# A tuned attention-and-expert kernel: one transpose moved from TensorE to DMA, one conversion moved ahead, loads issued one pair sooner, the last output split over two banks

## Chip, cores, metric

One core of one Trainium2 chip. The metric is device microseconds of one launch. The kernel before takes 212.0 us (median of 3 runs, 211.11 to 213.35). The profiled execution of it has a span of 209.9 us and took 211.65 us, so about 1.8 us lie outside the span.

A run is called slow here if it took over 1.5% more than the fastest run of the same kernel. Ratios are the mean time of one kernel's fast runs over that of the other's fast runs of the same rounds, so they are not quite the ratio of the medians that I quote.

## The reference, cut to what matters

```python
# q, k, v: 4 batches x 8 heads x 768 steps x 64
for t in range(S):
    state = gamma * state + k[:, :, t] (x) v[:, :, t]
    y[:, :, t] = scale * q[:, :, t] @ state
x = y.transpose(0, 2, 1, 3).reshape(3072, 512)
h = x @ w_in                     # 512 x 2048
out = (h * cos(h)) @ w_out       # 2048 x 512
```

## The kernel before

The 768 steps are cut into 6 chunks of 128. A *pair* p is one chunk of two batches; there are 12 pairs (p = 0 to 11; the "fourth pair" is p = 3). Two pairs make one group g of 512 tokens for the two large products. The parts that matter:

```python
SLOT = [0, 1, 2, 3, 2, 4, 0, 1, 3, 2, 4, 0]      # buffers of q, k, v by pair

def conv_q(p, eng): ...    # q * decay -> bf16, on VectorE or GpSimd
def conv_k(p, True): ...   # k -> bf16, on ScalarE
def conv_v(p, eng): ...    # v * decay -> bf16

def stage_t(p, b):         # 8 TensorE transposes into a PSUM bank, one VectorE copy
def stage_t_dma(p):        # the same by DMA, issued from SP
    for b in range(2):
        nc.sync.dma_start_transpose(out=qkt[n][:, b]..., in_=qk[n][:, b]...)

def attend(p):             # scores: matmuls on the transposed q and k (L215), then mask (L223)
def stage_y(p):            # outputs and state of the pair (L236, L241, L257)
def pair_f / unit_f        # x @ w_in, cosine on ScalarE, product on VectorE (L296, L284)
def unit_o(g, j, part)     # @ w_out (L310), copied by ScalarE, sent by SP

# ... pairs 2 and 3:
conv_k(2, True); conv_q(2, nc.vector)
#     ... stage_t(2, 0); stage_t(2, 1); conv_v(2, nc.vector); attend(2) between unit_o ...
conv_k(3, True); conv_q(3, nc.gpsimd)
load(nc.sync, 4, ("q0", "q1"));       load(nc.gpsimd, 4, ("k0", "k1", "v0", "v1"))
conv_v(3, nc.gpsimd)
load(nc.sync, 5, ("q0", "q1", "v0")); load(nc.gpsimd, 5, ("k0", "k1", "v1"))
#     ... stage_t(3, 0); stage_t(3, 1); attend(3) ...
stage_t_dma(4); load(nc.sync, 6, q); load(nc.gpsimd, 6, k and v)
#     ... stage_t_dma(5) ...
def later(p):
    stage_y(p)
    if p + 3 < NP: load(nc.sync, p + 3, q); load(nc.gpsimd, p + 3, k and v)
```

q goes out on SP's queue, k and v on GpSimd's. Pairs 0 to 3 are transposed by TensorE, pairs 4 to 11 by DMA.

## Time and profile before

| what | before |
|---|---|
| time, span | 212.0 us, 209.9 us |
| TensorE busy | 202.4 us (96%) |
| TensorE waits on a DMA of qkt (the transposed q and k) | none |
| DMA transposes | 16, 2.7 to 8.7 us from issue to landing |
| granted clock | 1.00 |

In the views below, a line of waits reads: engine and line, what it waited for, us in total, times, longest us. A timeline line reads: start, duration, engine, line, operation, count, and in brackets the idle time before it and what ended it. "SPq" is SP issuing a DMA: its duration is the time of issuing, not of the transfer. A DMA-issue line gives the count and the median us from issue to landing. In a line of stretches come the stretch, its length, busy us (and instructions) of TensorE, its weight loads, VectorE, ScalarE and GpSimd, then the granted clock, the DMA share and GB/s.

### The profile page before, as it was taken

Reading aid. Unit: us, or ns where it says so; the run is one execution under the profiler, and the core shown is the slowest. Engines: PE = TensorE matmul, PEld = TensorE weight load, DVE = VectorE, ACT = ScalarE, POOL = GpSimd, SP = SyncE. Lnnn points to the kernel's source line nnn. Section 1 sums busy time; section 2 is a strip of 40 time slices with the busy share of each in tenths; the row PEclk is TensorE's granted clock in tenths of the full one; section 3 lists DMA queues with packets and bytes.
Section 4 is the critical chain, followed back from the end, with each engine's and each line's share of the span. In section 5 each row is a group of like instructions: output and inputs, shape, how many; then the busy total and the mean of one; then the engine's idle time right before and its main releaser. Section 6 shows DMA issues by size and latency. Waiting matters only on the chain.

```text
span 209.9 us, 4164 instructions
## 1 busy us (share of the span) xinstructions
PE 202.4 (96%) x1637; PEld 112.3 (54%) x1637; DVE 115.5 (55%) x190; ACT 111.8 (53%) x181; POOL 91.4 (44%) x105
## 2 busy tenths in 40 slices
PE   7799999999999999999999999999999999999992
PEld 3258554548898555555455455455455444444440
DVE  4694785372967746859585385385482333443000
ACT  6267783227898337766845735735545554553120
POOL 7998238499995952999980700000000000000000
PEclk9999999999999999999999999999999999999999
DMA  6999999999799999999999171181101101110121
GB/s 154 340 247 207 216 260 288 338 265 349 177 217 237 218 307 283 182 290 227 288 115 273 53 103 52 50 103 50 50 3 50 50 4 50 50 50 27 74 88 65
DMA packets 49124, 33.83 MB, mean 161 GB/s; under 512 B 40080, under 2 KB 42384, under 8 KB 49104
## 3 DMA queue, kind: packets, MB, share of 16 engines
q1 hardware_dynamic: 42192, 15.86, 34.5%
q0 software_dynamic: 6768, 17.57, 31.8%
q8 instruction: 13, 0.21, 0.4%
q10 hardware_dynamic: 144, 0.13, 0.2%
q14 instruction: 7, 0.06, 0.1%
HBM read 27.26 MB, written 6.29 MB: 160 GB/s over the span
## 4 chain that ended last, share of the span: by engine, by line
PE 89%; POOL 3%; DMA 3%; DVE 2%; issue 1%; ACT 0%; POOLq 0%; DVEq 0%
PE bank L310 39%; PE bank L284 32%; PE bank L296 9%; DMA w_in<-in_moe_w_in_dram 3%; PE bank L236 3%; PE bank L215 3%; PE bank L241 2%; POOL vf L113 2%; POOL kf L113 1%; PE st_ps L257 1%; DVE vs L168 1%; PE bank L189 1%; DVE qkt L179 1%; POOL qf L113 0%; DVE am L223 0%
## 5 line engine op out<-in xcount | busy, mean ns | idle before, releaser
L279 DVE TENSOR_TENSOR gt<-bank,cosb 128x512 bf16<-128x512 f32 x96 | 65.7, 690 | 64.1 <-ACT cosb L275 63.7
L275 ACT ACTIVATE cosb<-bank,halfpi 128x512 bf16<-128x512 f32 x96 | 65.6, 688 | 52.3 <-PE bank L284 46.7
L310 PE MATMUL bank<-w_out_sb,gt 128*128 128x512 bf16 x384 | 93.3, 379 | 0.0
L284 PE MATMUL bank<-xt,w_in 128*128 128x512 bf16 x304 | 75.1, 380 | 0.0
L310 PEld LDWEIGHTS <-gt 128*128 128x128 bf16 x384 | 36.7, 98 | 42.8
L284 PEld LDWEIGHTS <-w_in 128*128 128x128 bf16 x304 | 33.8, 114 | 30.8 <-issue 0.2
L223 DVE TENSOR_TENSOR am<-bank,mask 128x512 bf16<-128x512 f32 x48 | 30.2, 681 | 0.3 <-PE bank L215 0.2
L163 POOL TENSOR_TENSOR qk<-qf,gq 128x512 bf16<-128x512 f32 x18 | 18.7, 1061 | 17.9 <-DMA qf<-in_q_dram 15.7
L322 ACT COPY ob<-bank 128x512 f32<-128x512 f32 x23 | 13.4, 587 | 22.6 <-PE bank L310 22.5
L168 POOL TENSOR_TENSOR vs<-vf,gk 128x512 bf16<-128x512 f32 x22 | 22.5, 1044 | 0.1
L113 POOL DMA_DIRECT2D vf<-in_v_dram x23 | 20.3, 886 | 5.0 <-DMA w_out_sb<-in_moe_w_out_dram 5.0
L113 POOL DMA_DIRECT2D kf<-in_k_dram x23 | 20.8, 906 | 2.0 <-DMA w_out_sb<-in_moe_w_out_dram 1.2
L174 ACT CAST qk<-kf 128x512 bf16<-128x512 f32 x24 | 13.9, 615 | 11.4 <-DMA kf<-in_k_dram 11.2
L296 PE MATMUL bank<-xt,w_in 128*128 128x256 bf16 x160 | 18.7, 273 | 0.6 <-ACT xt L245 0.4
L296 PEld LDWEIGHTS <-w_in 128*128 128x128 bf16 x160 | 17.1, 114 | 1.4 <-DMA w_in<-in_moe_w_in_dram 0.5
L245 ACT CAST xt<-bank 128x512 bf16<-128x512 f32 x24 | 13.0, 587 | 3.0 <-DVE gt L279 3.0
L241 PE MATMUL bank<-am,vs 128*64 128x128 bf16 x192 | 11.8, 220 | 0.7 <-POOL vs L168 0.7
L241 PEld LDWEIGHTS <-vs 128*64 128x64 bf16 x192 | 9.9, 110 | 2.1 <-POOL vs L168 1.7
L236 PEld LDWEIGHTS <-stb 128*64 128x64 bf16 x160 | 8.6, 109 | 4.0 <-issue 3.5
L236 PE MATMUL bank<-qkt,stb 128*64 128x128 bf16 x160 | 10.6, 222 | 0.0
L262 DVE CAST stb<-st_ps 64x512 bf16<-64x512 f32 x12 | 8.2, 687 | 3.5 <-PE st_ps L257 3.3
L332 PE MATMUL bank<-gt 128*128 128x512 bf16 x21 | 8.4, 514 | 1.2 <-DVE gt L140 1.2
(36 smaller groups left out, 66.1 us busy)
## 6 DMA issues: line engine op xcount, KB each, us to landing
kf<-in_k_dram POOLq DMA_DIRECT2D x23, 256.0 KB, 6.0
vf<-in_v_dram POOLq DMA_DIRECT2D x23, 256.0 KB, 7.0
out_dram<-ob SPq DMA_DIRECT2D x23, 256.0 KB, 2.0
qf<-in_q_dram SPq DMA_DIRECT2D x19, 256.0 KB, 6.7
w_in<-in_moe_w_in_dram POOLq DMA_DIRECT2D x4, 512.0 KB, 7.8
w_out_sb<-in_moe_w_out_dram POOLq DMA_DIRECT2D x4, 512.0 KB, 12.3
qf<-in_q_dram POOLq DMA_DIRECT2D x5, 256.0 KB, 7.4
kf<-in_k_dram SPq DMA_DIRECT2D x1, 256.0 KB, 4.7
```

Source lines behind the costliest of these rows:

```text
L113: eng.dma_start(out=t[SLOT[p]][b], in_=src[2 * bp + b, :, ds(c * C, C)].rearrange("h t d -> t h d"))
L163: eng.tensor_tensor(out=qk[p % NB][:, b, 0], in0=qf[SLOT[p]][b], in1=bc(gq, p % NC), op=ALU.mult)
L168: eng.tensor_tensor(out=vs[p % NB][:, b], in0=vf[SLOT[p]][b], in1=bc(gk if g is None else g, p % NC), op=ALU.mult)
L174: nc.scalar.copy(out=qk[p % NB][:, b, 1], in_=kf[SLOT[p]][b])
L223: nc.vector.tensor_tensor(out=am[p % 2][b][j], in0=ap[j], in1=mask.unsqueeze(1).to_broadcast([128, HP, 128]), op=ALU.mult)
L236: nc.tensor.matmul(yp[ts(j, 64), a, :], lhsT=stb[p % 2][:, b, a, ts(j, 64)], rhs=qt(n, b, a), start=True, stop=False, skip_group_check=True)
L241: nc.tensor.matmul(yp[ts(j, 64), a, :], lhsT=vs[n][:, b, 2 * a + j, :], rhs=am[p % 2][b][j][:, a, :], start=(c == 0), stop=True, skip_grou ...
L275: nc.scalar.activation(out=cb, in_=bank, func=AF.Sin, bias=halfpi)
L279: nc.vector.tensor_tensor(out=out, in0=bank, in1=cb, op=ALU.mult)
L284: nc.tensor.matmul(bank, lhsT=w_in_t(i, f), rhs=xt[g % 2][:, i, :], start=(i == 0), stop=(i == KIN - 1))
L296: nc.tensor.matmul(bank[:, ts(e, 256)], lhsT=w_in_t(i, f + e), rhs=xt[g % 2][:, i, ts(hf, 256)], start=(i == 0 and e == 0), stop=(i == KIN ...
L310: nc.tensor.matmul(bank, lhsT=gt[g % 2][:, f, ts(j, 128)], rhs=w_out_sb[:, f, :], start=(f == 0), stop=(f == KOUT - 1))
```

## The change

The intent was to take work and waits off TensorE, and to give the loads more lead. Four parts:

```diff
 # part 4: the last output, in place of halves of one bank copied one after the other
+    def last_o(g, j):
+        for i, (a, n) in enumerate(((0, 320), (320, 192))):
+            bank = banks.take()
+            ... 16 matmuls of n columns ...
+            # i = 0: ScalarE copies, SP sends; i = 1: VectorE copies, ScalarE's queue sends
 # part 2: third pair's v ahead of its transposes
     conv_q(2, nc.vector)
+    conv_v(2, nc.vector)
...
-                conv_v(2, nc.vector)        # was behind stage_t(2, 1)
 # part 1: fourth pair by DMA
     conv_q(3, nc.gpsimd)
+    stage_t_dma(3)
     load(nc.sync, 4, ("q0", "q1"))
...
-    stage_t(3, 0)
-    stage_t(3, 1)
 # part 3: loads from the eighth pair on one pair sooner
     stage_t_dma(5)
+    load(nc.sync, 7, ("q0", "q1"))
+    load(nc.gpsimd, 7, ("k0", "k1", "v0", "v1"))
...
-        if p + 3 < NP:
-            load(nc.sync, p + 3, ("q0", "q1"))
-            load(nc.gpsimd, p + 3, ("k0", "k1", "v0", "v1"))
+        if p + 4 < NP:
+            load(nc.sync, p + 4, ("q0", "q1"))
+            load(nc.gpsimd, p + 4, ("k0", "k1", "v0", "v1"))
```

More of the change, by code (lines that the diff above doesn't have):

```diff
@@ L315, in unit_o @@
             dst = out[ds((2 * bp + j % 2) * S + c * C, C), :]
-            if g == NG - 1 and j == 3:
-                nc.vector.tensor_copy(out=o[:, ts(0, 256)], in_=bank[:, ts(0, 256)])
-                nc.sync.dma_start(out=dst[:, ts(0, 256)], in_=o[:, ts(0, 256)])
-                nc.scalar.copy(out=o[:, ts(1, 256)], in_=bank[:, ts(1, 256)])
-                nc.scalar.dma_start(out=dst[:, ts(1, 256)], in_=o[:, ts(1, 256)])
-            else:
-                nc.scalar.copy(out=o, in_=bank)
-                nc.sync.dma_start(out=dst, in_=o)
-            banks.give(bank)
+            nc.scalar.copy(out=o, in_=bank)
+            nc.sync.dma_start(out=dst, in_=o)
+            banks.give(bank)
+    def last_o(g, j):
+        bp, c = divmod(2 * g + j // 2, NC)
+        dst = out[ds((2 * bp + j % 2) * S + c * C, C), :]
+        for i, (a, n) in enumerate(((0, 320), (320, 192))):
+            bank = banks.take()
+            for f in range(KOUT):
+                nc.tensor.matmul(bank[:, :n], lhsT=gt[g % 2][:, f, ts(j, 128)],
+                                 rhs=w_out_sb[:, f, ds(a, n)],
+                                 start=(f == 0), stop=(f == KOUT - 1))
+            o = ob[i]
+            if i:
+                nc.vector.tensor_copy(out=o[:, :n], in_=bank[:, :n])
+                nc.scalar.dma_start(out=dst[:, ds(a, n)], in_=o[:, :n])
+            else:
+                nc.scalar.copy(out=o[:, :n], in_=bank[:, :n])
+                nc.sync.dma_start(out=dst[:, ds(a, n)], in_=o[:, :n])
     spare = banks.take()
@@ L472 @@
             if g > 2:
-                unit_o(g - 1, *divmod(s, 4))
+                if g < NG or s < 12:
+                    unit_o(g - 1, *divmod(s, 4))
+                elif s == 12:
+                    last_o(g - 1, 3)
             if p < NP:
```

## The prediction

> **What bounds the kernel now.** I read the page's busy line first, then the chain of waits, then TensorE's own waits, then the timeline of the stage that the change touches. The page says:
>
> ```profile
> span 209.9 us, 4164 instructions
> PE 202.4 (96%) x1637; PEld 112.3 (54%) x1637; DVE 115.5 (55%) x190; ACT 111.8 (53%) x181; POOL 91.4 (44%) x105
> PE 89%; POOL 3%; DMA 3%; DVE 2%; issue 1%; ACT 0%; POOLq 0%; DVEq 0%
> ```
>
> TensorE is busy for 96% of the span and holds 89% of the chain that ended last; no other engine is past 55%. The rest of the chain lies in three places: 15.6 us at the start (loads until w_in lands, which the change leaves alone), a VectorE piece between 40.0 and 44.0 us, and the end. So only TensorE work taken away, or TensorE waits taken away, can shorten this kernel. TensorE's waits, longest first, are few:
>
> ```profile
> PE bank L332 <- DVE gt L140: 1.2, 1, 1.2
> PE bank L241 <- POOL vs L168: 0.7, 1, 0.7
> PE bank L296 <- ACT xt L245: 0.4, 1, 0.4
> PE bank L215 <- DVE qkt L179: 0.4, 1, 0.4
> PE bank L215 <- DVE am L223: 0.4, 1, 0.4
> ...
> PE bank L296 <- DMA w_in<-in_moe_w_in_dram: 0.2, 1, 0.2
> ```
>
> From 60 us to 206.2 us the same view is empty. Whatever the change does to loads there can bring TensorE nothing; it can only take something away.
>
> The timeline of 36 to 60 us shows the third pair (p=2):
>
> ```profile
> 40.03 1.29 DVE L179 TENSOR_SCALAR qkt<-bank 128x512 uint32<-128x512 uint32 x2 [5.15 <-PE bank L189]
> 41.23 2.13 DVE L168 TENSOR_TENSOR vs<-vf,gk 128x512 bf16<-128x512 f32 x2
> 43.29 2.47 DVE L223 TENSOR_TENSOR am<-bank,mask 128x512 bf16<-128x512 f32 x4
> 43.39 0.23 PE L215 MATMUL bank<-qkt 64*128 64x128 bf16 x1
> 44.02 0.38 PE L215 MATMUL bank<-qkt 64*128 64x128 bf16 x7 [0.40 <-DVE am L223]
> ```
>
> VectorE copies the transposed q and k, then converts v for 2.13 us, and only then masks. The second batch's scores (L215) start at 43.39, and their second matmul waits to 44.02 for a bank that the mask frees. And the chain, listed in order of time, has the fourth pair's transposes as TensorE time of their own:
>
> ```profile
> 51.08 0.89 PE bank L189 x16
> ```
>
> **What the Trainium skill says.** "TensorE: Matmul & The Clock Gate", Part 4: PE-mode transpose: its output goes to PSUM, so a copy follows. Agreed: each batch's 8 transposes are followed by one L179 copy of 684 ns. Its figure of about 275 ns per transpose is not the cost in a stream; here 16 take 0.89 us, 56 ns each. "SBUF — State Buffer", Who interferes with whom: a VectorE instruction with two SBUF inputs contends with a GpSimd one that reads SBUF. Agreed: the two conversions of v on VectorE took 682 and 1533 ns, the longer while GpSimd converted q (1283 ns against a median of 1049). "PSUM — Partial Sum Buffer", PSUM bank collisions raise a hardware error: two engines may not touch one bank's quadrant at once, even reading. That is why the two halves of the last output are copied one after the other before; two banks allow both. "DMA: Bandwidth & Descriptors", DMA Transpose (X-bar): 2-byte data, from SP or ACT; both hold here. The trace gives the time: 2.8 to 8.0 us from issue to landing.
>
> **The change, part by part.**
>
> 1. Fourth pair by DMA. Goes: 16 transposes, 0.89 us of TensorE, all on the chain, and two VectorE copies (2 x 0.68 us) with no TensorE wait of their own. Comes: two DMA transposes ahead of the loads of pairs 4 and 5 on SP's queue. Their inputs: k converted at 41.2 us, q at 42.8 us. Needed: the fourth pair's scores ran at 53.7, so about 52.1 now. With 1.25 us per issue and the trace's 2.8 to 8.0 us they land at about 46 to 51: in time. **-0.89 us.**
>
> 2. v of the third pair ahead of T. v's two loads were issued at 26.46 and 29.37 and took 10.9 and 8.7 us: landed at 37.4 and 38.1. Two conversions of 0.68 us then end at about 38.8, before the transposes' copy at 40.03. The masks start right after the scores (about 41.6), two end by 43.0, and banks are free when TensorE comes at 43.4. From there to the next w_out group (44.40) it took 1.01 us where 8 score matmuls need 0.28 (half of 0.55 for 16). **-0.73 us.**
>
> 3. Loads sooner from the eighth pair on: no TensorE wait lies there, so **0**.
>
> 4. The last output in two banks, of 320 and 192 columns. TensorE: the same 16 x 512 columns at 0.42 ns each (3.46 us), as the weight loads stay hidden even at 128 columns (56 ns a transpose). Before: copy on VectorE from 206.23 to 206.67, copy on ScalarE from 206.69 to 207.06, then the last transfer is issued (207.09). After: the first bank is copied and sent while TensorE makes the second, and one VectorE copy of 192 columns is left (about 0.36 us, an estimate from 425 ns for 256 and 690 for 512). 0.86 - 0.40 = **-0.46 us.**
>
> Sum: 0.89 + 0.73 + 0.46 = 2.08 us, of 212.0: 209.9, or 1.0%.
>
> **The rivals.**
>
> *A: SP's queue falls behind, and pair 4's or 5's transpose arrives late.* Issues on SP keep their order. Before, pairs 4 and 5's q went out while SP had nothing else to do:
>
> ```profile
> 33.85 9.57 SPq L113 DMA_DIRECT2D qf<-in_q_dram  x4
> 43.46 0.78 SPq L113 DMA_DIRECT2D vf<-in_v_dram  x1
> 46.02 4.63 SPq L323 DMA_DIRECT2D out_dram<-ob  x4
> 55.02 3.47 SPq L198 DMA_TRANSPOSE qkt<-qk  x2
> ```
>
> They took 9.57 us to issue, for the queue was full (landing after 6 to 10 us, 16 engines at a share of 1.0 throughout). Now they stand behind a transpose that waits for pair 3's conversions until 41 to 43 us. Moved by 8 to 10 us, with the free stretch of 50.65 to 55.02 to absorb 4.4 of it and less competition from GpSimd's queue to absorb some more, pair 4's transpose goes out at 55 to 58 instead of 55.02. It landed at 61.5 and 64.5 (6.5 and 8.0 us), and pair 4's scores started at 66.39: 1.9 us of slack, of which parts 1 and 2 use 1.6. Pair 5 is alike: landed at 68.6 and 69.5, scores at 71.77. Any delay here becomes a TensorE wait before L215. For it: those numbers, and the busy DMA. Against: GpSimd's loads of pair 3 lose a competitor and come 1 to 2 us sooner, so the transpose of pair 3 too. I give a visible loss even odds, of 0.3 to 2 us, about 0.7 on average: 210.2 to 212.
>
> *B: v lands after the transposes are done.* VectorE works in order, so v landing past 39.4 would hold up the copy. In the trace it landed 1.3 us sooner. One chance in ten; up to 1 us lost, 210.9.
>
> *C: the extra transposes and earlier loads take DMA time from pairs 6 to 8.* Pair 6's transposes landed at 70.5 and 71.6 for scores at 79.59; pair 7's at 87.8 for 91.61; pair 8's at 100.6 for 104.89: 4 to 8 us of slack. Pair 7's q was what GpSimd waited 5.7 us for at 76 to 82, and that gets better. Unlikely to cost anything: 209.9.
>
> *D: the gain is larger, because waits that I count once ripple.* With no wait after 60 us, nothing is there to ripple: 209.5 at best.
>
> **Range and chances.** 209.9 if nothing is late, less than half a microsecond more for rival A on average: **210.2 us**. Low end 208.9: all parts, and a run as good as the lowest before (211.1 - 2.1 = 209.0). High end 211.8: A takes nearly all of it. Faster by over 2% means under 207.8, twice my sum: 0.03. Slower by over 2% means over 216.2, a wait of over 6 us that the range of landings does not give: 0.02. Within 2%: 0.95.
>
> **What would show each step.** Part 1: L189 matmuls 48 instead of 64, L179 copies 6 instead of 8, 18 DMA transposes instead of 16, and no TensorE wait at pair 3's scores at about 52. Part 2: VectorE's v conversion at 37 to 39, masks right after the scores, no wait on the mask. Part 3: GpSimd's waits for q down from 15.7 us, no TensorE wait changed. Part 4: from TensorE's last matmul to the last issue about 0.5 us instead of 0.95. Rival A: TensorE waiting on a DMA of qkt at 64 to 72. The prediction is wrong if TensorE waits there for more than 2 us, or if its busy time falls by clearly more or less than 0.9 us.

## The result

The changed kernel took 221.76 us (median of 4 runs: 223.49, 226.01, 220.03, 219.47) against 211.76 us of the kernel before in the same rounds (4 runs, 211.11 to 213.35). The ratio of fast runs is 1.0366 (95% interval 1.0264 to 1.0468): slower by 3.7%. The fast runs alone show it, at 219.5 and 220.0 us. The profiled run is the one of 223.49 us, a slow one by the rule above.

The page of the changed kernel: span, busy line, granted clock in 40 slices (a 9 is 0.9 or more), and the engines' shares of the chain that ended last.

```profile
span 221.6 us, 4171 instructions
PE 205.7 (93%) x1637; PEld 113.9 (51%) x1637; DVE 114.3 (52%) x188; ACT 111.8 (50%) x181; POOL 91.3 (41%) x105
PEclk9999999999999789995999999999999999999999
PE 55%; DMA 13%; POOL 1%; SPq 1%; issue 1%; DVE 0%; DVEq 0%; POOLq 0%
```

TensorE's share of the chain fell from 89% to 55%, and DMA's rose from 3% to 13%. TensorE's waits in the changed kernel, the first two:

```profile
PE bank L215 <- DMA qkt<-qk: 9.8, 6, 3.1
PE bank L343 <- DVE gt L140: 1.2, 1, 1.2
```

The first line is new: six waits of the scores on a DMA transpose, 9.8 us in all. The timeline of TensorE has them at pairs 4, 5 and 7, two batches each:

```profile
65.27 0.40 PE L215 MATMUL bank<-qkt 64*128 64x128 bf16 x8 [0.47 <-DMA qkt<-qk]
67.16 0.40 PE L215 MATMUL bank<-qkt 64*128 64x128 bf16 x8 [1.50 <-DMA qkt<-qk]
...
74.17 0.40 PE L215 MATMUL bank<-qkt 64*128 64x128 bf16 x8 [1.79 <-DMA qkt<-qk]
74.95 0.40 PE L215 MATMUL bank<-qkt 64*128 64x128 bf16 x8 [0.39 <-DMA qkt<-qk]
...
99.41 0.61 PE L215 MATMUL bank<-qkt 64*128 64x128 bf16 x8 [3.09 <-DMA qkt<-qk]
102.57 0.61 PE L215 MATMUL bank<-qkt 64*128 64x128 bf16 x8 [2.55 <-DMA qkt<-qk]
```

So 2.0 us at pair 4, 2.2 at pair 5, 5.6 at pair 7. SP's own timeline, to be held against the one in the prediction, shows what stands in front of pair 4's transpose:

```profile
41.16 2.75 SPq L198 DMA_TRANSPOSE qkt<-qk  x2
44.02 6.28 SPq L113 DMA_DIRECT2D qf<-in_q_dram  x4
...
51.98 3.79 SPq L317 DMA_DIRECT2D out_dram<-ob  x4
55.94 5.38 SPq L198 DMA_TRANSPOSE qkt<-qk  x2
```

The fourth pair's transpose itself is early enough (issued at 41.16 and 42.68, landed at 44.0 and 47.1; no wait at its scores). q of pairs 4 and 5 goes out about ten microseconds later. Pair 4's transpose has two halves, one for each batch. The first goes out only 0.9 us later than before (55.94 for 55.02), but takes 9.3 us to land, where it took 6.5. The second goes out 2.1 us later (58.66 for 56.54) and takes 8.5 us, where it took 8.0. So the first is late mainly by its flight, the second mainly by its issue.

Pair 7 lost its time in both places too. Its k was converted by 85.24 and its q by 85.47, but SP came to its transpose only at 91.42, behind an output and two loads of pair 9's q:

```profile
81.24 4.29 SPq L317 DMA_DIRECT2D out_dram<-ob  x1
85.58 5.68 SPq L113 DMA_DIRECT2D qf<-in_q_dram  x2
91.42 6.47 SPq L198 DMA_TRANSPOSE qkt<-qk  x2
```

That is 5.9 us in SP's queue. Its halves then took 7.9 and 5.9 us to land, where they took 3.8 and 2.8 before. No run separates the two for pair 7.

Two parts came out as predicted. VectorE's timeline in the changed kernel: v is converted while VectorE had been idle, and the masks follow the copies at once, with no wait on the mask at TensorE:

```profile
37.69 1.46 DVE L168 TENSOR_TENSOR vs<-vf,gk 128x512 bf16<-128x512 f32 x2 [2.44 <-DMA vf<-in_v_dram]
39.93 1.29 DVE L179 TENSOR_SCALAR qkt<-bank 128x512 uint32<-128x512 uint32 x2 [0.78 <-PE bank L189]
41.56 1.29 DVE L223 TENSOR_TENSOR am<-bank,mask 128x512 bf16<-128x512 f32 x2 [0.35 <-PE bank L215]
```

And the end of the changed kernel: ScalarE's copy of 320 columns is long done when VectorE's of 192 ends the kernel.

```profile
217.36 0.42 ACT L334 COPY ob<-bank 128x320 f32<-128x320 f32 x1 [1.63 <-PE bank L326]
...
218.69 0.36 DVE L331 COPY ob<-bank 128x192 f32<-128x192 f32 x1 [13.36 <-PE bank L326]
219.08 0.37 ACTq L332 DMA_DIRECT2D out_dram<-ob  x1
```

From the start of the last copy to the last issue it takes 0.39 us, where it took 0.86 (206.23 to 207.09).

The clock adds to the loss. After two of the stalls the granted clock falls; two stretches of the changed kernel:

```profile
72.00:84.00 12.00, 9.83 (x98) 4.76 (x92) 3.86 (x6) 2.92 (x6) 10.60 (x12) 0.86 0.97 194
100.00:108.00 8.00, 5.45 (x26) 2.35 (x25) 2.08 (x4) 1.34 (x2) 4.76 (x5) 0.62 1.19 245
```

The clock's deficit is 0.14 x 12 + 0.38 x 8 = 4.7 us in these two. A part of that falls into the waits themselves and costs nothing more, so it is an upper bound. The account closes within it: 209.9 - 2.1 (predicted gains) + 9.8 (waits) = 217.6, and 221.6 was measured; the 4.0 us left are within the 4.7. TensorE's busy time agrees: 0.9 us of work left it, and yet it rose from 202.4 to 205.7 us, 4.2 us more than that work would give.

### The profile page after: what moved, and what is told of

It reads as the page before. It is cut to its first block, busy times and chain, and to the rows that moved or that the text cites.

```text
span 221.6 us, 4171 instructions
## 1 busy us (share of the span) xinstructions
PE 205.7 (93%) x1637; PEld 113.9 (51%) x1637; DVE 114.3 (52%) x188; ACT 111.8 (50%) x181; POOL 91.3 (41%) x105
## 2 busy tenths in 40 slices
DMA packets 51236, 34.36 MB, mean 155 GB/s; under 512 B 42192, under 2 KB 44496, under 8 KB 51216
## 3 DMA queue, kind: packets, MB, share of 16 engines
q0 software_dynamic: 6768, 17.57, 29.8%
## 4 chain that ended last, share of the span: by engine, by line
PE 55%; DMA 13%; POOL 1%; SPq 1%; issue 1%; DVE 0%; DVEq 0%; POOLq 0%
PE bank L310 27%; PE bank L284 22%; DMA qkt<-qk 5%; DMA out_dram<-ob 4%; DMA qf<-in_q_dram 3%; PE bank L326 2%; PE bank L236 1%; PE bank L215 1%; PE bank L241 1%; SPq L198 1%; POOL qk L163 1%; POOL vs L168 1%; PE st_ps L257 0%; SPq L113 0%; DVE ob L331 0%
## 5 line engine op out<-in xcount | busy, mean ns | idle before, releaser
L310 PE MATMUL bank<-w_out_sb,gt 128*128 128x512 bf16 x368 | 92.3, 388 | 0.0
L310 PEld LDWEIGHTS <-gt 128*128 128x128 bf16 x368 | 35.6, 99 | 42.6 <-issue 2.9
L168 POOL TENSOR_TENSOR vs<-vf,gk 128x512 bf16<-128x512 f32 x22 | 22.5, 1044 | 15.9 <-PE st_ps L257 15.8
L163 POOL TENSOR_TENSOR qk<-qf,gq 128x512 bf16<-128x512 f32 x18 | 18.6, 1046 | 10.5 <-PE st_ps L257 4.5
L174 ACT CAST qk<-kf 128x512 bf16<-128x512 f32 x24 | 14.0, 615 | 11.4 <-DMA kf<-in_k_dram 11.2
L215 PE MATMUL bank<-qkt 64*128 64x128 bf16 x192 | 8.9, 225 | 10.2 <-DMA qkt<-qk 9.8
L215 PEld LDWEIGHTS <-qkt 64*128 64x128 bf16 x192 | 5.6, 97 | 15.4 <-DMA qkt<-qk 11.2
## 6 DMA issues: line engine op xcount, KB each, us to landing
w_out_sb<-in_moe_w_out_dram POOLq DMA_DIRECT2D x4, 512.0 KB, 12.5
```

The source lines that it names most:

```text
L163: eng.tensor_tensor(out=qk[p % NB][:, b, 0], in0=qf[SLOT[p]][b], in1=bc(gq, p % NC), op=ALU.mult)
L168: eng.tensor_tensor(out=vs[p % NB][:, b], in0=vf[SLOT[p]][b], in1=bc(gk if g is None else g, p % NC), op=ALU.mult)
L174: nc.scalar.copy(out=qk[p % NB][:, b, 1], in_=kf[SLOT[p]][b])
L215: nc.tensor.matmul(ap[j][:, a, :], lhsT=kt(n, b, a)[po : po + 64, :], rhs=qt(n, b, a)[po : po + 64, :], tile_position=(po, 0))
L310: nc.tensor.matmul(bank, lhsT=gt[g % 2][:, f, ts(j, 128)], rhs=w_out_sb[:, f, :], start=(f == 0), stop=(f == KOUT - 1))
```

## The experiments

Two theories stood. **Q**: the order on SP's queue (part 1 holds back q of pairs 4 and 5). **L**: the earlier loads (part 3) are the cause. Rivals came up on the way: **D**, that one more transpose or more traffic is too much for the DMA engines in any order, **O**, that loads right behind a transpose on its own queue delay it, and **K** or **M**, that a DMA transpose lands late when loads of *GpSimd's* queue are in flight beside it. All kernels gave correct results. The first four shared one chip, the next four another set of rounds, and so on; "before" beside each is from the same rounds. The waits in the last column are those of the one profiled run, which was a slow one in e1, e5, e6, e7, e10 and e15.

| run | edit to | median us (runs, range) | before | ratio, 95% | TensorE waits on qkt, profiled run |
|---|---|---|---|---|---|
| e1 | part 1 alone | 216.9 (4, 213.2-218.5) | 211.9 | 1.0119 (1.0037-1.0200) | 5.1 us, pair 4 |
| e2 | part 3 alone | 219.0 (4, 216.6-220.7) | 211.9 | 1.0244 (1.0178-1.0310) | 2.9, pair 5 |
| e3 | parts 1, 2, 4 | 213.2 (4, 211.4-217.8) | 211.9 | 1.0027 (0.9964-1.0091) | 2.3, pair 4 |
| e4 | parts 2, 4 | 210.9 (6, 210.7-212.2) | 211.9 | 0.9962 (0.9920-1.0003) | none |
| e5 | part 3, k and v only | 217.7 (20, 211.3-225.0) | 211.7 | 1.0012 (0.9959-1.0065) | 4.3, pairs 5, 6 |
| e6 | part 3, q only | 220.7 (4, 217.5-225.2) | 211.7 | 1.0327 (1.0200-1.0454) | 5.1, pairs 6, 7 |
| e7 | 1, 2, 4; transpose of pair 3 behind the loads | 220.1 (4, 215.3-222.3) | 211.7 | not given | 6.5, pairs 3, 4 |
| e8 | all, with filling matmuls | 226.7 (4, 226.2-227.3) | 211.7 | 1.0694 (1.0623-1.0765) | 4.5, pair 4 |
| e9 | before, extra transfers | 212.5 (1) | 211.6 | none (one look) | none |
| e10 | 1, 2, 4; transpose of pair 3 between q loads | 215.5 (6, 209.9-220.6) | 211.6 | not given | 8.0, pair 4 |
| e11 | part 3 on one queue | 213.0 (5, 212.2-214.1) | 211.6 | 1.0069 (1.0036-1.0103) | 0.7 |
| e12 | 1, 2, 4; all loads on one queue | 216.8 (6, 216.4-218.1) | 212.2 | 1.0226 (1.0182-1.0270) | 1.3, pair 4 |
| e13 | e10, pair 6 on on one queue | 212.2 (22, 211.0-214.6) | 212.1 | 1.0019 (0.9988-1.0050) | none |
| e14 | e4 again | 210.7 (19, 210.5-218.7) | 212.1 | 0.9958 (0.9933-0.9983) | none |
| e15 | e13, k of pair 6 later | 213.9 (6, 212.6-217.2) | 211.6 | 1.0100 (1.0052-1.0148) | none |

### e1: part 1 alone

```diff
     conv_q(3, nc.gpsimd)
+    stage_t_dma(3)
     load(nc.sync, 4, ("q0", "q1"))
...
-    stage_t(3, 0)
-    stage_t(3, 1)
```

> Only the fourth pair's transpose by DMA (loads, v and the last output as before). Theory Q (order on SP's queue: the transpose of pair 3 holds the q loads of pairs 4 and 5 behind it, so pair 4's and 5's transposes land late): 0.9 us saved, 2 to 4 us of TensorE waits on a DMA of qkt at 64 to 75 us, so 213 to 216 us, and no wait at pair 7's scores. Theory L (the earlier loads are the whole cause): no such wait, 211 us.

Measured: 216.9 us, waits of 5.1 us, all at pair 4, none at pair 7. In the profiled run (217.97 us, a slow one) pair 4's transpose was issued at 57.45 and 59.88 and landed only after 12.5 and 11.3 us. L alone falls. The size is uncertain: the ratio of fast runs is 1.0119, and its interval starts at 1.0037.

### e2: part 3 alone

```diff
     stage_t_dma(5)
+    load(nc.sync, 7, q); load(nc.gpsimd, 7, k and v)
...
-        if p + 3 < NP:
+        if p + 4 < NP:          # and p + 3 -> p + 4 in both loads
```

> Only the loads from the eighth pair on issued one pair sooner. Theory Q: they stand ahead of pair 6's and 7's transposes but those have 4 to 8 us of slack, so 212 us (within 0.5%), GpSimd's waits for q shorter. Theory L: TensorE waits on a DMA of qkt at pair 7's scores (about 5 us there in the changed kernel), 216 to 221 us.

Measured: 219.0 us, ratio 1.0244. Both theories missed: the loads alone do cost time, against Q, but in this run the wait is 2.9 us at pair 5, not at pair 7. Pair 5's transpose is *ahead* of all the moved loads on SP's queue. Its second half, as SP issued it and as it landed; first the kernel before, then e2:

```profile
65.26 1.24 SPq L198 DMA_TRANSPOSE qkt<-qk  x1
DMA to landing us min/median/max: 4.2/4.2/4.2
```
```profile
65.35 2.63 SPq L198 DMA_TRANSPOSE qkt<-qk  x1
DMA to landing us min/median/max: 9.8/9.8/9.8
```

Issued within 0.1 us of the same moment, it landed 5.7 us later. What differs around it: before, GpSimd issued nothing from 58.55 to 69.30 us (it converted q and v of pairs 5 and 6, and waited 2.7 us for q of pair 6), and in e2 it issues k and v of pair 7 from 62.72 to 66.27. This is what K and M were formed on.

### e3: parts 1, 2 and 4

The edit is the whole change without part 3.

> The changed kernel with its loads put back (parts 1, 2 and 4). Theory Q: waits at pairs 4 and 5 remain (about 4 us, plus 1 to 2 us of lower clock after them), the 5.6 us at pair 7 is gone or below 1 us, 213 to 216 us. Theory L: all waits gone, 209.7 us. Rival D (DMA time: the extra transposes themselves load the engines, whatever the order): waits at pairs 4, 5 and 7 all remain at about half, 215 to 218 us.

Measured: 213.2 us, nearest to Q, which had expected about 4 us of waits at pairs 4 and 5: 2.3 us of wait at pair 4, none at pairs 5 and 7, and the clock lower right after (0.50 from 70 to 72 us). Without part 3 the loss is mostly gone, so part 3 carries most of it. By fast runs this kernel equals the one before.

### e4: parts 2 and 4

The edit is the whole change without parts 1 and 3.

> The two parts that touch no queue: v of the third pair ahead of T, and the last output in two banks. All theories: 0.73 + 0.46 = 1.2 us saved, 210.6 us against 211.8; mask wait at 44 us gone, 0.5 us instead of 0.95 from the last matmul to the last issue. No TensorE wait on a DMA of qkt (there is no slack taken that pair 4 does not have: 1.9 us against 0.73).

Measured: 210.9 us, span 208.9 against 209.9, no wait on a transpose or a mask. The repeat, e14, narrows the ratio to 0.9958 (0.9933 to 0.9983): a gain clear of the noise.

### e5 and e6: which of the moved loads

```diff
 # e5                                            # e6
     stage_t_dma(5)
+    load(nc.gpsimd, 7, k and v)                 +    load(nc.sync, 7, q)
...  # later(p): k, v at p + 4, q at p + 3        # q at p + 4, k, v at p + 3
```

> Part 3 for k and v alone (GpSimd's queue): pair 7's k and v right after pair 5's transpose, q at the old time. In the run of part 3 alone the second half of pair 5's transpose was issued at 65.35 us as before (65.26), but took 9.8 us instead of 4.2; q of pair 7 is behind it on SP's queue. Theory K (k and v of pair 7 on GpSimd's queue compete with the transpose on the DMA engines): wait of 2 to 4 us at pair 5's scores stays, 215 to 218 us. Theory O (q of pair 7, right behind the transpose on the same queue, disturbs it): no wait, 212 us.

> Part 3 for q alone (SP's queue). Theory K: pair 5's transpose takes 4 to 6 us to land, no or under 1 us of wait at its scores, 212 us. Theory O: wait of 2 to 4 us there, 215 to 218 us.

e5: the profiled run (a slow one, 219.2 us) has 3.9 us of wait at pair 5, whose second half was issued at 64.79 and landed after 11.4 us. But 3 of its 20 runs are as fast as before, and the ratio of fast runs is 1.0012. What changed is how often a run is late (17 of 20 slow, against none of 23 before), and the rule about slow runs lets me draw no size from that. e6: pair 5's transpose landed after 5.2 and 4.4 us, without a wait, as K has it. The time went to 220.7 us all the same, because pairs 6 and 7's transposes landed after 6.0 to 10.8 us. Pair 7's also stood in SP's queue, as in the changed kernel: its inputs were converted by 81.14, and it was issued at 88.11, behind an output and two loads of q. So K is right for pair 5, O is not; K's "212 us" was wrong, since I had thought of pair 5 alone.

### e7 and e10: the transpose of pair 3 elsewhere on SP's queue

```diff
 # e7: behind the loads of pairs 4 and 5         # e10: between q of pair 4 and q of pair 5
-    stage_t_dma(3)                              -    stage_t_dma(3)
     load(nc.sync, 4, ...)                            load(nc.sync, 4, ("q0", "q1"))
     load(nc.sync, 5, ...)                       +    stage_t_dma(3)
     load(nc.gpsimd, 5, ...)
+    stage_t_dma(3)
```

> Parts 1, 2 and 4, but the fourth pair's transpose is issued on SP after the loads of pairs 4 and 5, not ahead of them. Theory Q (order on SP's queue): q of pair 4 goes out at 34 us again, pair 4's transpose is issued at about 54 and lands by 62, its wait (2.3 us before) is gone; the fourth pair's own transpose is issued at 44 to 47 and lands at 49 to 52, in time for its scores at 52 or up to 1 us late; 210 us. Theory D (DMA time of one more transpose, whatever its place): pair 4's scores still wait about 2 us, 212 to 214 us.

> Parts 1, 2 and 4 with the fourth pair's transpose between the q loads of pair 4 and those of pair 5 on SP's queue. Theory Q (what counts is that pair 4's q is not held back): transpose of pair 3 issued at about 41 and landed by 48, pair 4's at 54 to 55 and landed by 63, no TensorE wait, 209.9 us. Theory M (any transpose that meets GpSimd's loads is late by chance): runs spread from 210 to 217 us, with waits at pair 4 or 5.

e7: 220.1 us. The fourth pair's own transpose, issued at 44.68 and 47.38, took 12.2 and 12.1 us to land and cost 6.1 us at its scores. Q's expectation of 49 to 52 us was wrong. e10: 215.5 us with runs from 209.9 to 220.6. q of pair 4 went out at 34.10 and pair 4's transpose at 54.62, about as before the change (33.85 and 55.02), and yet that transpose took 12.5 and 16.6 us. **Q falls as the cause for pair 4**: with the order put right the lateness stays. For pair 7 in the changed kernel the order did cost time (5.9 us in SP's queue, above). M's expectation, a spread from 210 to 217, is what came, a little wider.

### e8: the changed kernel with filling matmuls

```diff
         bk = [banks.take(), banks.take()]
+        for _ in range({(4, 0): 2, (4, 1): 7, (5, 0): 8, (5, 1): 2,
+                        (7, 0): 14, (7, 1): 12}.get((p, b), 0)):
+            nc.tensor.matmul(bk[0], lhsT=w_in_sb[0][:, 0, :128], rhs=w_in_sb[0][:, 0, :], ...)
```

> The changed kernel with 45 matmuls of 128x512 (9.7 us) put where TensorE stood waiting for pairs 4, 5 and 7 (their results are overwritten). If the lower granted clock (0.977) comes from TensorE standing idle: clock 1.00, the waits on a DMA of qkt about 1 us, time 216 to 219 us against 222, although no work is taken away. If the clock has nothing to do with the idle time: 222 us or more at 0.98.

Measured: 226.7 us, so the expected time was wrong. The filling delayed the work that the next transposes wait for, and pair 4 still stood for 4.5 us. But the clock answers. Where the filling covered the stall (pair 7), the stretch that had 0.62 in the changed kernel reads, in e8:

```profile
100.00:108.00 8.00, 8.00 (x45) 3.58 (x42) 3.53 (x6) 2.61 (x5) 6.83 (x8) 1.00 1.08 237
```

Where TensorE still stood (pair 4), it fell to 0.61 from 68 to 72 us. So the lower clock follows TensorE's standing idle; in these runs it is a consequence of the waits and not a second cause.

### e9: the transfers measured by themselves

Extra transfers, used by nobody, in the quiet stretch of the kernel before (from 161 us on). A one-column-block copy on GpSimd that reads a fresh product holds all groups but the fourth back until their turn.

```diff
+            if g == NG - 1 and s == 1:   gate(0, 0); stage_t_dma(0)
+            elif g == NG - 1 and s == 4: gate(1, 3); extra_loads(nc.gpsimd)
+            elif g == NG - 1 and s == 8: gate(1, 7); extra_loads(nc.gpsimd); stage_t_dma(1)
+            elif g == NG - 1 and s == 12: extra_loads(nc.sync); stage_t_dma(2)
+            elif g == NG and s == 0:     gate(0, 15); extra_loads(nc.gpsimd); stage_t_dma(0)
```

> The kernel before, with extra transfers whose results nobody uses, in the quiet stretch from 161 us on: a pair's two DMA transposes alone; then four loads of k and v on GpSimd's queue alone; then the same four loads and two transposes together; then four loads and two transposes one behind the other on SP's queue; then loads on GpSimd's queue and transposes together once more. Theory M (a DMA transpose and GpSimd's loads in flight together hold each other up): alone the transposes land in about 2.8 to 4.5 us and the loads within 7; together the transposes take 8 us or more and the throughput falls to about 100 GB/s, below that of either alone; on one queue no such fall. Theory D (they merely share the DMA engines' time): together the transposes take at most 6 to 7 us, and the throughput stays above 180 GB/s, that of transposes alone.

The DMA issues of the transposes in the four stretches of e9, in order: alone; beside four loads of GpSimd's queue; behind four loads on SP's own queue; beside loads of GpSimd's queue once more (with outputs being sent too).

```profile
qkt<-qk SPq DMA_TRANSPOSE x2, 2.7
...
qkt<-qk SPq DMA_TRANSPOSE x2, 5.4
...
qkt<-qk SPq DMA_TRANSPOSE x2, 4.3
...
qkt<-qk SPq DMA_TRANSPOSE x2, 10.2
```

2.7 us alone, 4.3 behind the same four loads on the same queue, 5.4 and 10.2 beside GpSimd's. The first mixture is within what D allows (6 to 7 us), and it tells little: four loads and two transposes took 8.6 us from the first issue to the last landing beside each other (180.04 to 188.68), and 9.1 us one behind the other (186.93 to 196.07). The second mixture is beyond D, but it also met outputs and the end of the transposes before it. The expected fall of the throughput to 100 GB/s is not general: it was 212 and 181 GB/s over the two mixtures, and near 100 only from 200 to 202 us (94 GB/s). So e9 alone does not decide between M and D, and M's "throughput falls below that of either alone" is not shown by it.

### e11 and e12: the same loads on one queue

```diff
 # e11: part 3's earlier loads, all on SP, each pair's behind a transpose
     stage_t_dma(5)
+    load(nc.sync, 7, ("q0", "q1", "k0", "k1", "v0", "v1"))
...
     stage_t_dma(6)
+    load_all(8)
...
                         stage_t_dma(p + 1)
+                        load_all(p + 3)
 # e12: parts 1, 2, 4; all loads from pair 4 on on SP, pairs 7 on behind a transpose (p + 2)
```

> Part 3's earlier loads, but k and v too from pair 7 on go out on SP's queue, each pair's six loads right behind a transpose, so that no transpose meets a load of GpSimd's queue after 70 us. Theory M: pair 5's transpose lands by 70 us (75.1 in the run of part 3 alone), no or under 1 us of wait at its scores, clock 1.00, 211.5 to 213 us with a spread of 2 us. Theory D or O (the amount of traffic, or loads right behind on the same queue, is what delays): waits of 3 us and more stay, 215 to 220 us.

> Parts 1, 2 and 4, with all loads from pair 4 on (q, k and v) on SP's queue, those of pairs 7 and on right behind a transpose, each at least one transpose later than in the changed kernel. If the lateness comes from transposes in flight beside loads of GpSimd's queue: transposes land within 6 us of their issue, waits on a DMA of qkt under 1 us, clock 1.00, and the gains of parts 1, 2 and 4 show: 209.5 to 210.5 us, runs within 2 us of each other. If one more transpose is too much for the DMA engines in any order: waits of 2 us and more at pairs 4 and 5, 212 us and more.

e11: 213.0 us against e2's 219.0, five runs within 2 us of each other, clock 1.00. TensorE's waits on transposes in e11:

```profile
PE bank L215 <- DMA qkt<-qk: 0.7, 2, 0.4
```

The bytes are the same, and pair 5's transpose landed at 69.5 and 70.5. So neither the amount of traffic by itself (D) nor loads right behind the transpose on its own queue (O) delays it. But two things differ from e2, not one: the queue of k and v, and their time. In e2 GpSimd issued pair 7's k and v from 62.72 us on, beside the transpose; in e11 SP issues them from 69.68 on, behind it, and they land 2.5 to 7.2 us later. No run separates the two. The traces together point to the queue. Of the 297 transposes recorded in the 17 traces, 142 had no load of GpSimd's queue in flight in the first 2.7 us after their issue, and the longest of these took 5.6 us, even with four to six transfers of SP's own queue in flight (16 cases, 5.5 us at most). Of the 102 that had four or more of GpSimd's loads beside them, 73 took over 6 us, up to 17.5. e11 is still 0.7% above the kernel before (ratio 1.0069), so the earlier loads bring nothing here either.

e12: all 18 transposes landed within 2.7 to 4.4 us (median 2.9), the runs agree within 1.7 us. But the time is 216.8: pair 4's transpose now stands behind twelve loads and four outputs, is issued at 61.5, and its scores wait 1.3 us, with 2.8 us more where TensorE waits for VectorE's product. The landing was as expected, the waits, the clock (0.984) and the time were not. What the one queue cost here is issue: pair 4's transpose went out at 61.5, where the changed kernel had it out at 55.9.

### e13, e14, e15: does part 1 pay once nothing lies beside the transposes?

```diff
 # e13: e10, and pair 6's six loads on SP behind pair 4's transpose, the later ones behind theirs
     stage_t_dma(4)
-    load(nc.sync, 6, q); load(nc.gpsimd, 6, k and v)
+    load(nc.sync, 6, ("q0", "q1", "k0", "k1", "v0", "v1"))
 # e15: e13 with pair 6's loads behind stage_t_dma(5), conv_k(6) and stage_t_dma(6) behind later(4)
```

> As the run with the transpose of pair 3 between the q loads of pairs 4 and 5 (210 to 221 us, pair 4's transpose issued at 54.6 and landed after 12.5 and 16.6 us), but k and v of pair 6 and later go out on SP's queue behind pair 4's, 6's and the later transposes. If GpSimd's loads in flight beside the transpose were the cause: pair 4's transpose is issued at 54 to 56 and lands within 6 us, no wait on a DMA of qkt over 1 us, clock 1.00, 209.5 to 211.5 us with a spread of 2 us. If one more transpose is too much in any company: pair 4's or 5's scores still wait 2 us and more, 213 us and more.

> Parts 2 and 4 alone once more: 210.9 us as before, 0.4 to 0.6% below the kernel before on the same chip, no wait on a DMA of qkt, spread of 2 us.

> As e13, with pair 6's loads behind pair 5's transpose on SP's queue, and pair 6's k converted on ScalarE after the output of pair 4 instead of ahead of the last cosines. If the wait of ScalarE for k was what was left: transposes of pairs 4 and 5 land before their scores at 65 and 70 us, no TensorE wait over 1 us after 40 us, clock 1.00, 209.5 to 210.5 us, below parts 2 and 4 alone (210.7). If something else limits it: 212 us as e13.

The DMA issues around pair 4's transpose (54.7 to 58.5 us; the median of its two halves), first e10, then e13:

```profile
qkt<-qk SPq DMA_TRANSPOSE x2, 14.6
```
```profile
qkt<-qk SPq DMA_TRANSPOSE x2, 6.2
```

Issued at 54.62 in the one and 54.68 in the other; e10's landed after 14.6 us, e13's after 6.2, and e13 has no TensorE wait on a transpose at all. So in e10 pair 4 was late for GpSimd's loads of pair 6, which went out from 55.05 on, beside the transpose; in e13 they go out on SP from 60.65 on, behind it. Again queue and time moved together. That one more transpose is too much in any order (D) falls with e13, too. The expected 6 us was missed by 0.9 for the first half (6.9). What the DMA engines did from 60 to 72 us, first e10, then e13 (the last two numbers are their share and GB/s):

```profile
60.00:72.00 12.00, 5.55 (x56) 5.11 (x53) 5.93 (x11) 6.49 (x11) 2.67 (x3) 0.86 1.12 118
```
```profile
60.00:72.00 12.00, 10.17 (x95) 7.40 (x94) 7.08 (x12) 7.07 (x13) 4.09 (x4) 0.99 0.99 209
```

In e10 they were as busy and moved little more than half, and GpSimd's four loads were late too: 10.5 to 15.9 us, where the same four took 6.0 to 6.8 before.

The time, 212.2 us, is that of the kernel before and no better. The wait has gone elsewhere; two lines of e13's timeline:

```profile
66.19 0.62 ACT L174 CAST qk<-kf 128x512 bf16<-128x512 f32 x1 [2.38 <-DMA kf<-in_k_dram]
...
70.44 0.22 PE L241 MATMUL bank<-am,vs 128*64 128x128 bf16 x1 [0.95 <-DVE am L223]
```

k of pair 6 is later on SP's queue; ScalarE, working in order, waits 2.4 us for it ahead of the cosines, so products and masks come late and TensorE waits for the masks. The clock fell here too (0.60 from 72 to 76 us), although no single gap was longer than 0.95 us: TensorE had been busy for 2.22 of the 4 us before. e15 moved that conversion: pairs 4 and 5's scores were undelayed (5.37 us apart, as before), but 213.9 us came out. In its profiled run (217.2 us, a slow one) TensorE waits 2.5 us for a product of VectorE at 84 us, with the clock lower after it, and 4.0 us at the transposes of the first two pairs, before 16 us, which the edit does not touch. Whether every load on SP can be early enough for ScalarE is left open.

The best kernel measured is e4, parts 2 and 4: 210.7 to 210.9 us, below both kernels.

## Why the prediction was wrong

- **What bounds it**: right. TensorE set the end, and the loss is TensorE waiting.
- **Part 1, -0.89 us**: the transposes left TensorE, and the fourth pair's landed in time (44.0 and 47.1). Right for that pair. The prediction's own sign, TensorE's busy time down by 0.9 us, failed: it rose by 3.3, through the clock. e1 shows the part costs more than it brings.
- **Part 2, -0.73 us, and part 4, -0.46 us**: right in mechanism, a little large in size. Together 1.2 us predicted; e4's span is 1.0 us shorter, its ratio 0.9962, e14's 0.9958, some 0.9 us. No run parts the two; the traces show 0.47 us for part 4 (0.86 to 0.39). Rival B (v lands late) did not come: v was converted from 37.69 on.
- **Part 3, "no TensorE wait lies there, so 0"**: this is the step that failed most. e2 makes it +2.4%. An empty list of waits tells that nothing is late *now*, not how much room is left. I had asked only what earlier loads could bring, a shorter wait of GpSimd for q, and had not seen that GpSimd's silence from 58.55 to 69.30 us was the stretch in which pairs 5 and 6's transposes flew: its last load before it landed at 64.46.
- **Rival A**: its place (pairs 4 and 5), its sign and its slack of 0.3 us were right, its cause only in part. It laid the delay to the order on SP's queue. In the changed kernel that accounts for 0.9 us of the 3.7 by which the first half of pair 4's transpose landed later, and for 2.1 of the 2.6 of the second; but e10 kept the order right and was late all the same. It put the size at 0.3 to 2 us; the changed kernel has 4.2 us at pairs 4 and 5. The failed term is the landing time: I took 2.8 to 8.0 us from the trace as a property of the transpose, and it was one of its company. (The trace's own range is 2.7 to 8.7; pair 9's halves, at 8.7 and 8.5 us, were left out.) Beside GpSimd's loads it took up to 17.5 us in the runs (e7).
- **Rival C, "unlikely to cost anything"**: wrong. Pair 7, with 3.7 us of slack, was late by 5.6: 5.9 us passed in SP's queue before its issue, and the flights took 3 to 4 us more than before.
- **Not in the prediction at all**: the clock, up to 4.7 us on top. e8 ties it to TensorE's idle time.
- **The chances**: slower by over 2% got 0.02, because I bounded the delay with the range of landings of one profile of a kernel that had been tuned around it. Another profile of the same code was wider: in e9, which up to 161 us is the kernel before, transposes took 10.2, 10.9 and 11.0 us, and TensorE waited for none.

What stays open: why a transpose is late beside GpSimd's loads, and whether it is their queue or only their being in flight at that moment. The page before gives GpSimd's queue 17.57 MB in 6768 packets (2.6 KB each, worked out) and SP's 15.86 MB in 42192 (376 bytes each). If the engines took packets in turn, the small ones would get little of the time. But then GpSimd's loads should gain what the transpose loses, and in e10 both were late and the sum fell to 118 GB/s. So this is not the whole of it; no run varied the size of packets. Open too is how much of the changed kernel's spread comes from it and how much from the chip.

## What to carry to other kernels

A hole in one DMA queue may be what lets another queue's transfers land in time: before filling it, look at what is in flight there, and take the slack of each consumer (landing against use), not the list of waits. Read a transfer's duration together with what ran beside it. When a transfer is late, change its company and its place in the queue in separate runs, as the cause may be either.

## What the Trainium skill lacked or had wrong

- "DMA: Bandwidth & Descriptors", Rules for kernel authors, says that a transpose next to ordinary DMAs needs nothing. The results were correct in every run, so that holds for correctness. For time it lacks a warning: 2.7 us alone (e9), 5.4 and 10.2 us beside loads of GpSimd's queue, and up to 16.6 us in e10 and 17.5 in e7. With all loads on SP's queue, 2.7 to 4.4 us (e12).
- "TensorE: Matmul & The Clock Gate", Why this matters for your kernels, asks for no idle gaps over about 3 us. In e3 a wait of 2.3 us was followed by a granted clock of 0.80, 0.50 and 0.85 in the next three stretches of 2 us. In e13 three gaps of 0.30, 0.95 and 0.38 us between 68.9 and 71.0 us were followed by 0.60 from 72 to 76. So in this kernel shorter gaps were enough, though not always: after the 2.0 us at pair 4 in the changed kernel it stayed at 1.00 to 74 us.
- The same page, Part 4, gives about 275 ns for a TensorE transpose in another kernel, and nothing for a stream of them. Here the record of one lasts 219 ns (median), and 16 in a stream took 0.89 us, 56 ns each.
